# Booking SyncE's DMA issues at other lengths, and other distances for long transfers, in a kernel that plans its own order

## The chip, the cores and the metric

The kernel runs on one core of one Trainium2 chip. The metric is the device time in microseconds (us), and the median of several runs is given. One further execution is profiled; every duration of a single instruction comes from that one. The names of the engines are those of the profile: PE is the matmul engine (PEld its weight loads), DVE the vector engine, ACT the scalar engine, POOL the general-purpose engine, SP the engine that only issues DMA transfers. A "q" behind a name (SPq) means the engine's instruction queue.

## The reference

Two blocks follow one another: a delta-rule attention over 768 time steps for 4 batches x 8 heads of width 48, and a gated feed-forward network on its output.

```python
k_n = k / (np.linalg.norm(k, axis=-1, keepdims=True) + 1e-06)
state = np.zeros((B, H, D, D), dtype=np.float32)
for t in range(S):
    kt, vt, bt = (k_n[:, :, t], v[:, :, t], beta[:, :, t, None])
    y[:, :, t] = np.einsum('bhd,bhde->bhe', q[:, :, t], state)
    v_old = np.einsum('bhde,bhd->bhe', state, kt)
    state = state + bt[:, :, :, None] * np.einsum('bhd,bhe->bhde', kt, vt - v_old)
...
x = attn_out.transpose(0, 2, 1, 3).reshape(B * S, H * D)      # 3072 x 384
rms = np.sqrt(np.mean(x * x, axis=-1, keepdims=True) + 1e-06)
xn = x / rms * rms_g
g = xn @ w_gate                                               # 384 x 1536
silu = g * (1.0 / (1.0 + np.exp(-g)))
val = xn @ w_val
return (silu * val @ w_out).astype(np.float32)                # 1536 x 384
```

## The kernel before, in words

The sequence is cut into 12 chunks of 64 steps. For each chunk there are four kinds of work.

- `load` brings in `k`, `q` and `v` of the chunk. `weights` brings in the three weight matrices once, in 18 pieces of 768 KB, in the first quarter of the time; the core holds them as float32 after a conversion on ACT and DVE.
- `prep` makes the chunk's triangular inverse. The products of keys (L555, L662) go out to device memory as `dkk` and come back in another layout as `at`; `at` is scaled (L682) and combined (L709 to L719); a chain of 15 pairs of DVE instructions (L731, L737) inverts it; the result `acc` goes out as `dx` and `dxt` and comes back as `mt`, `x2bd` and `m1bd`; two merges on PE (L813, L837) finish it. For chunks 0 to 3 the scaling is done on DVE, after that on POOL.
- `recur` takes the state forward one chunk and makes the chunk's output `yn`: products with the state (L878), with the inverse (L924), with the masked scores (L938), the new state (L975), then the root mean square (squares L1012 on ACT, the power on POOL at L1024 and L1025, the scaling on ACT at L1040) and a transposition (L1046).
- `ffn` is the feed-forward network of the chunk: for chunks 0 and 1 in plain form (up L1118, down L1100), for the ten others in a form with fewer products (up L1211, with DVE L1221 and ACT L1223 and L1227 behind it; down L1268, with DVE L1260 and L1277), and at the end the stores of 96 KB from `tmp` to the output.

All of it, over all chunks, is put into one list of operations (class `Op`) before a single instruction is emitted. Each has an engine, a duration that the author booked, what it reads and writes, and a priority. The class `Plan` then looks for an order: `forward` plays the list through with these durations, engine by engine, always taking the operation that can start first; `backward` goes from the end to the start and sets new priorities from how late each operation may be; random shakes are added. This is done 110 times (`ROUNDS`), the order with the earliest planned end is kept, and the instructions are emitted in it. Each engine executes its instructions strictly in that order; across engines only data dependences hold one up. So a booked duration never takes time itself: it only decides in which place of its engine's queue an instruction stands.

A DMA transfer is an operation of SP (in the startup some are ACT's): `dur` is the time that the issue is booked for on SP, `work` the time that the transfer is booked for on the DMA engines, which `forward` treats as one server. A transfer is either short, that is, part of a chain that other work waits for (`dkk`, `at`, `dx`, `mt` and the like), or `bulk` (loads of inputs and weights). From the second round on, the planner knows when the short ones were issued in the round before (`op.past`), and holds a bulk transfer back if it would come too close ahead of one:

```python
if op.bulk:
    for t, _ in soon:
        if t >= max(server, s + FIRST) + clear * op.work:
            break
        if t > s:
            s = t + 0.01
```

`clear` is the factor from `CLEAR`; the rounds take its three values in turn (`CLEAR[k % len(CLEAR)]`). On PE, the first 62 us are filled up with matmuls of no use (L1368) between the real ones.

Of the kernel before, what the change touches and what calls it, by code (L numbers as in the profile page):

```python
# [28 lines left out]
SHAKE = 0.06  # L29
RING, LANES, FIRST, LAND = 2330, 8, 1.08, 0.9  # L30
WARM = 62.0
CLEAR = (1.0, 0.6, 1.4)


class Op:
# [249 lines left out]
def kernel(  # L285
# [57 lines left out]
    NK, NKQ = 3, 2  # L343
    k2 = sbt("k2", [128, 16, DP], NK)
    q2 = sbt("q2", [128, 16, DP])
    q2t = q2.rearrange("p x e -> p (x e)").rearrange("p (u g th e) -> p u g th e", u=8, g=2, th=2)
    q2k = [("q2", i) for i in range(16)]
    vt = sbt("vt", [128, 16, D])
# [38 lines left out]
    raw = [more[:, 1536 * i : 1536 * i + 1536].bitcast(I64) for i in range(NRAW)]  # L387
# [7 lines left out]
    dkk = [dram.tile([2, 2, 16, W, W], FP32, name=f"dkk{i}") for i in range(2)]  # L395
    dx = [dram.tile([2, 2, 16, W, W], FP32, name=f"dx{i}") for i in range(2)]
# [5 lines left out]
    A = lambda n: 0.2 + 0.0008 * n  # L402
    G = lambda n: 0.15 + 0.0022 * n

    def dma(dst, src, prio, r=(), w=(), work=0.2, dur=0.45, eng="SP", after=0.0, desc=256, bulk=False):
        queue = nc.scalar if eng == "ACT" else nc.sync
        op = P.add(eng, dur, lambda: queue.dma_start(out=dst, in_=src), prio, r, w, lat=0.1)  # L407
        op.dma, op.work, op.ready, op.desc, op.bulk = True, work, after, desc, bulk
        op.port = False
# [55 lines left out]
    def weights():  # L465
        todo = []
        for half_ in range(2):
            c0 = half_ * WCOL

            for i_ in range(3):  # L470
                for side, (key, w) in enumerate((("wg", moe_w_gate), ("wv", moe_w_val))):
                    c1 = c0 + 256 * i_
                    src = w.rearrange("(t p) c -> p t c", p=128)[:, :, c1 : c1 + 256]
                    todo.append((w_in[:, side, half_, i_:9:3], src, [(key, half_, i_)]))
                if i_:
                    for f in ((6 * half_,) if i_ == 1 else (6 * half_ + 2, 6 * half_ + 4)):
                        src = moe_w_out[f * 128 : f * 128 + 256, :].rearrange("(a p) c -> p a c", a=2)
                        z = spot(f)
                        todo.append((wo_sb[:, z : z + 2], src, [("wo", f), ("wo", f + 1)]))
        for n, (dst, src, keys) in enumerate(todo):  # L480
            pr = (30 if n < 9 else CV2) + 0.2 * n
            i, a = n % NRAW, n % NCV
            parts = dst.shape[1]
            rdst = raw[i].rearrange("p (a c) -> p a c", a=parts)
            dma(rdst, src, (0.1 if n == 0 else 3 + 2 * n), w=[("raw", i)], dur=0.45, work=3.06, desc=384 if parts == 3 else 256, bulk=True)

            low, high = (raw[i].bitcast(U32)[:, w_ : w_ + 2 * WCOL - 1 : 2] for w_ in range(2))
            top, cc = cva[a], cvb[a]
            cak, cvk = [("cva", a)], [("o", 1)] if a else [("tmp", 1), ("tmp", 2)]
            u, r = top.bitcast(U32), cc.bitcast(U32)  # L490
            tiled = lambda t: t.rearrange("p (a n) -> p a n", a=parts)

            P.add("ACT", 0.84, lambda high=high, top=top: nc.scalar.activation(out=top, in_=high.bitcast(FP32), func=ACTF.Prelu, scale=2.0**-112, alpha=2.0**32), pr, r=[("raw", i)], w=cak)
            P.add("ACT", 0.84, lambda low=low, r=r: nc.scalar.mul(r, low, 2.0**-29), pr, r=[("raw", i)], w=cvk)
            P.add("DVE", 0.57, lambda u=u: nc.vector.tensor_scalar(out=u, in0=u, scalar1=3, scalar2=None, op0=ALU.logical_shift_left), pr, w=cak)
            P.add("DVE", 0.93, lambda dst=dst, u=tiled(u), r=tiled(r): nc.vector.tensor_tensor(out=dst.bitcast(U32), in0=u, in1=r, op=ALU.add), pr, r=cvk + cak, w=[("cv", n)])
            done = [("cv", n)]
            for key in keys:
                ready.setdefault(key, []).extend(done)
# [4 lines left out]
    def load(c, what):  # L504
        t0 = c * C
        pk, pq, pv = ((-5, 1, 12), (5, 29, 36))[c] if c < 2 else (due(c, 150), due(c, 99), due(c, 70))
        if "q" in what and c > 1:
            for d, eh, g, th in itertools.product(range(2), repeat=4):
                e0, e1 = 32 * eh, min(D, 32 * eh + 32)
                src = q.rearrange("b (yh a) t e -> a t (b yh) e", a=4)[2 * d + g, t0 + 32 * th : t0 + 32 * th + 32, :, e0:e1]  # L510
                r0 = 64 * d + 32 * eh
                dma(q2t[r0 : r0 + 32, :, g, th, 0 : e1 - e0], src, pq, w=[q2k[8 * d + 4 * eh + 2 * g + th]], work=0.21, bulk=True)
        for key, t, src, pr in (("k2", k2[c % NK], k, pk), ("q2", q2, q, pq)):
            for g in range(2):
                if key[0] not in what or key == "q2" and c > 1:
                    continue
                dst = t[64 * g : 64 * g + 64, :, 0:D]
                s = src.rearrange("b (y g) t e -> g t (b y) e", g=2)[g, t0 : t0 + C]
                dma(dst, s, pr, w=[(key, c % NK, g)] if key == "k2" else q2k[8 * g : 8 * g + 8], dur=0.65, work=1.15, desc=1024, eng="ACT" if c == 0 and g and key == "k2" else "SP", bulk=c > 0 or key == "q2")
        if "v" in what:  # L520
            for bb in range(2):
                s = v[2 * bb : 2 * bb + 2, :, t0 : t0 + C, :].rearrange("p h t e -> t (p h) e")
                dma(vt[64 * bb : 64 * bb + 64], s, pv, w=[("v", bb)], dur=0.65, work=1.15, desc=1024, bulk=True)

    def turn(src, dst, keys, r, pr, split):

# [76 lines left out]
    def prep(c):  # L603
        early = c < 2
        pr = 8.0 if c == 1 else due(c, 110)
        if c == 0:
            pr = 0.0
        pn = pr if early else due(c, 125)
        pd = pr + (1 if c else 0)
        pi = (1.0, 45.0)[c] if c < 2 else due(c, 80)  # L610
        i2, ikq, ikk, imt = c % 2, c % NKQ, 2 if c == 1 else c % 2, int(c == 1)
# [6 lines left out]
        eng, e_ = (nc.vector, "DVE") if fast else (nc.gpsimd, "POOL")  # L618
# [3 lines left out]
        if c == 0:  # L622
# [3 lines left out]
            for d in range(2):  # L626
                dst = kraw[:, d:16:2]
# [24 lines left out]
            pr = 6.0  # L652
# [6 lines left out]
        for d in range(2):  # L659
            dst = kk[ikk][:, :, d:16:2]  # L660
            src = lambda d=d, ps=ps: ps[d].t.rearrange("p (u i t) -> p i u t", u=8, i=2)
            P.add("ACT", A(512), lambda dst=dst, f=src: nc.scalar.mul(dst, f(), -1.0), pr, r=[ps[d]], w=kkd(d), last=ps[d])  # L662

        dk = dkk[c % 2]
        for g in range(2):
            for i in range(2):
                r0 = 64 * g + W * i
                src = kk[ikk][r0 : r0 + W, i] if c else kraw[r0 : r0 + W, :, W * i : W * i + W]
                kbkeys = [(("kka", ikk // 2, d), ("kkb", ikk, d))[i] if c else ("kr", d) for d in range(2)]
                dma(dk[i, g].rearrange("x j t -> j x t"), src, pd, r=kbkeys, w=[("dkk", c % 2, g, i)], work=0.43, dur=0.4, desc=512, eng="ACT" if c == 0 and g else "SP")  # L670
        dkeys = [("dkk", c % 2, g, i) for g in range(2) for i in range(2)]
        at_, an = (at2, "at2") if c == 1 else (at1, "at")
        atk = [(an, 0), (an, 1)]
        for par in range(2):
            dma(at_[64 * par : 64 * par + 64].rearrange("p j t -> p (j t)"),
                dk.rearrange("i g x j t -> (i g x) (j t)"), pd, r=dkeys, w=[(an, par)], dur=0.5, work=1.42, desc=64, eng="SP" if par or c else "ACT")
        bt = beta_b[:, c]
        bkeys = [("beta", i) for i in range(8)]

# [24 lines left out]
        x, xkeys = (xs_[c + 1], [("xs", c)]) if early else (xs_[0], ["acc"])  # L704
# [21 lines left out]
        for j in range(0, W - 2, 2):  # L726
            n, m = j // 2 + 1, W - 2 - j
# [32 lines left out]
        turns = itertools.cycle(("SP",) if c else ("ACT", "SP"))  # L760
        for par in range(2):
            dst = dx[i2].rearrange("i g x (s two) t -> two (i g x) s t", two=2)[par]
            dma(dst, x[64 * par : 64 * par + 64], pi, r=xkeys, w=[("dx", i2, par)], dur=0.6, work=0.9, desc=1024, eng=next(turns))
            if early:
                continue
            dst = dxt[i2].rearrange("t g x s -> (g x) t s")[:, :, 16 * par : 16 * par + 16]
            dma(dst, xt_[64 * par : 64 * par + 32], pi, r=["acc"], w=[("dxt", i2, par)], dur=0.65, work=0.67, desc=1024)
        xk = [("dx", i2, 0), ("dx", i2, 1)]
        xtk = [("dxt", i2, 0), ("dxt", i2, 1)]
        for i in range(2):  # L770
            for bb in range(2):
                r0 = 64 * bb + W * i
                for g in range(2):
                    src = dx[i2][i, g, 8 * bb : 8 * bb + 8].rearrange("x s t -> s x t")
                    dma(mt[imt][r0 : r0 + W, 8 * g : 8 * g + 8, W * i : W * i + W], src, pi, r=xk, w=[("mt", imt, i, bb, g)], eng=next(turns))
        for y_ in range(4):
            src = dx[i2][1].rearrange("g (b y) s t -> y s (g b) t", y=4)[y_]
            dst = x2bd[W * y_ : W * y_ + W, :, y_]
            dma(dst, src, pi, r=xk, w=[("x2bd", y_)], eng=next(turns))
        if early:  # L780
# [13 lines left out]
            for g in range(2):  # L794
                s = slice(64 * g, 64 * g + W)
                for bb in range(2):
                    src = lambda s=s, bb=bb: psm[bb].t[s, 0:256].rearrange("p (x s) -> p x s", s=W)
                    dst = m1bd[s, 8 * bb : 8 * bb + 8, g]
# [4 lines left out]
        else:  # L803
            for g in range(2):
                src = dxt[i2][:, g]
# [598 lines left out]
```

## Time and profile before

| | |
|---|---|
| median of 3 runs | 707.42 us (703.76 to 709.53) |
| the profiled execution | 708.47 us |
| its span, first to last instruction | 706.7 us |
| instructions | 23129 |
| PE busy | 688.2 us, 97% of the span |
| DVE busy | 538.7 us, 76% |
| ACT busy | 314.9 us, 45% |
| POOL busy | 138.2 us, 20% |
| mean granted clock of PE | 0.99 |
| DMA | 54.66 MB, mean 77 GB/s; 0.79 of the engines' time before 64 us, 0.62 from 64 to 190 us, 0.19 after 560 us |
| DMA issues on SP | 556 |

The span is the profiled execution without the 1.8 us that lie around it. Busy time is not added up over engines, since they work side by side. Engine SP has no busy time in the table: its issues are seen in the timeline and among the instructions of line L407, where every transfer is made. A wait is written as "who waited <- who ended the wait: total us, times, longest us". In the timeline a row has the start, the length, the engine, the line, what was written from what, and in brackets the idle time before it with what ended it.

### The profile page before, as it was taken

The page shows a single profiled execution, that of the slowest core. Times are in us where ns is not written, and L with a number is a line of the kernel's source. Part 1 is how long each engine was busy: PE and PEld are TensorE (multiplying, and loading weights), DVE is VectorE, ACT ScalarE, POOL GpSimd, SP SyncE. Part 2 cuts the span into 40 slices and gives each one's busy share as a digit, 9 for nine tenths or more (in the row PEclk, how much of TensorE's full clock was granted, in tenths as well). Part 3 has the DMA queues.
Part 4 walks back from the last instruction along what each step waited for, and adds up shares of the span by engine and source line. Part 5 has one row for each costly group of instructions (what it writes and reads, how often), then busy time and mean ns, then how long its engine had stood idle before and what let it go on. Part 6 is the DMA issues. An engine that isn't in the chain of part 4 may idle for free.

```text
span 706.7 us, 23129 instructions
## 1 busy us (share of the span) xinstructions
PE 688.2 (97%) x9924; PEld 628.1 (89%) x9924; DVE 538.7 (76%) x1121; ACT 314.9 (45%) x720; POOL 138.2 (20%) x140
## 2 busy tenths in 40 slices
PE   8998999999999989999999999999998999999997
PEld 6567768787789989999999999999998999999997
DVE  4896993599999739959957966979955988957373
ACT  5247573562235345345355254355354255345241
POOL 6020040030503005032106005042104131100000
PEclk9999999999999999999999999999999999999999
DMA  7975978821541361164352264253153061040101
GB/s 116 186 176 112 225 178 194 210 49 17 95 79 25 62 99 31 28 104 69 60 94 28 38 95 86 39 103 51 34 79 57 2 114 29 18 62 2 23 1 23
DMA packets 232790, 54.66 MB, mean 77 GB/s; under 512 B 221936, under 2 KB 225008, under 8 KB 232688
## 3 DMA queue, kind: packets, MB, share of 16 engines
q1 hardware_dynamic: 227840, 52.27, 39.5%
q8 instruction: 78, 1.28, 0.8%
q10 hardware_dynamic: 4848, 0.92, 0.7%
q14 instruction: 24, 0.20, 0.1%
HBM read 40.83 MB, written 12.32 MB: 75 GB/s over the span
## 4 chain that ended last, share of the span: by engine, by line
PE 75%; DVE 11%; SPq 6%; DMA 3%; issue 2%; POOL 1%; ACT 1%; DVEq 0%; ACTq 0%; POOLq 0%
PE bank L1211 31%; PE bank L1268 16%; PE bank L1118 9%; SPq L407 6%; PE bank L1100 3%; PE bank L878 3%; DVE acc L737 3%; PE bank L555 2%; DVE acc L731 2%; PE bank L924 2%; PE bank L938 2%; PE bank L837 1%; PE bank L532 1%; PE bank L975 1%; PE bank L1368 1%
## 5 line engine op out<-in xcount | busy, mean ns | idle before, releaser
L1211 PE MATMUL bank<-xf,w_in 128*128 128x128 f32 x1440 | 180.3, 277 | 2.4 <-ACT tmp L1223 2.2
L1221 DVE TENSOR_TENSOR tmp<-tmp,bank 128x512 f32<-128x512 f32 x180 | 122.2, 684 | 78.2 <-PE bank L1211 58.7
L1211 PEld LDWEIGHTS bank<-xf,w_in 128*128 128x128 f32 x1440 | 169.6, 192 | 5.2 <-ACT tmp L1223 2.4
L1211 PE MATMUL bank<-xf,more 128*128 128x128 f32 x960 | 125.2, 278 | 1.2 <-DVE tmp L1221 1.2
L1211 PEld LDWEIGHTS bank<-xf,more 128*128 128x128 f32 x960 | 116.1, 193 | 3.4 <-DVE tmp L1221 1.9
L1223 ACT COPY tmp<-bank 128x512 f32<-128x512 f32 x120 | 69.4, 585 | 69.0 <-PE bank L1211 39.9
L1227 ACT ACTIVATE tmp<-tmp 128x256 f32<-128x256 f32 x120 | 49.7, 417 | 105.2 <-DVE tmp L1221 104.7
L737 DVE TENSOR_REDUCE acc<-acc 128x30 f32<-128x90 f32 (+4 forms) x180 | 85.1, 473 | 6.2
L577 POOL TENSOR_TENSOR knrm<-ksum,half 128x16 f32<-128x16 f32 x12 | 36.1, 3009 | 157.1 <-DVE ksum L576 157.1
L1268 PE MATMUL bank<-wo_sb,hf 128*128 128x192 f32 x360 | 63.9, 327 | 0.2 <-ACT kt L544 0.2
L1228 DVE TENSOR_TENSOR hf<-tmp 128x256 f32<-128x256 f32 x120 | 51.4, 443 | 14.1 <-ACT tmp L1227 13.6
L731 DVE TENSOR_TENSOR acc<-acc,at 128x60 f32<-128x60 f32 (+4 forms) x165 | 58.2, 353 | 4.2 <-POOL at L714 1.7
L1268 PEld LDWEIGHTS bank<-wo_sb,hf 128*128 128x128 f32 x360 | 58.2, 190 | 0.7 <-ACT kt L544 0.5
L758 POOL COPY acc<-acc 128x128 f32<-128x128 f32 x40 | 18.2, 486 | 140.3 <-DVE acc L737 139.4
L1368 PE MATMUL bank<-ident 128*128 128x128 f32 (+2 forms) x148 | 43.5, 439 | 1.4 <-POOL ident masks.py:199 1.4
L1368 PEld LDWEIGHTS bank<-ident 128*128 128x128 f32 x148 | 25.0, 198 | 17.9 <-issue 15.4
L682 POOL TENSOR_TENSOR at<-at,beta_b 128x1024 f32<-128x1024 f32 x8 | 18.9, 2360 | 104.4 <-DMA q<-in_q_dram 49.5
L1100 PE MATMUL bank<-wo_sb,hf 128*128 128x384 f32 x96 | 34.0, 490 | 0.0
L1118 PE MATMUL bank<-xf,w_in 128*128 128x256 f32 x144 | 33.9, 385 | 0.0
L1118 PE MATMUL bank<-xp,w_in 128*128 128x256 f32 x144 | 33.6, 389 | 0.0
L1118 PEld LDWEIGHTS bank<-xp,w_in 128*128 128x128 f32 x144 | 28.1, 197 | 5.0
L1118 PEld LDWEIGHTS bank<-xf,w_in 128*128 128x128 f32 x144 | 26.7, 190 | 4.7 <-issue 0.2
(166 smaller groups left out, 997.3 us busy)
## 6 DMA issues: line engine op xcount, KB each, us to landing
at<-dkk SPq DMA_DIRECT2D x21, 256.0 KB, 4.0
vt<-in_v_dram SPq DMA_DIRECT2D x24, 192.0 KB, 4.1
more<-in_moe_w_val_dram SPq DMA_DIRECT2D x6, 768.0 KB, 8.2
more<-in_moe_w_gate_dram SPq DMA_DIRECT2D x6, 768.0 KB, 5.7
more<-in_moe_w_out_dram SPq DMA_DIRECT2D x6, 768.0 KB, 6.9
out_dram<-tmp SPq DMA_DIRECT2D x48, 96.0 KB, 2.2
k<-in_k_dram SPq DMA_DIRECT2D x23, 192.0 KB, 4.3
mt<-dx SPq DMA_DIRECT2D x84, 32.0 KB, 2.1
```

The costliest lines, as they stand in the source:

```text
L407: op = P.add(eng, dur, lambda: queue.dma_start(out=dst, in_=src), prio, r, w, lat=0.1)
L731: nc.vector.tensor_tensor(out=acc[:, 1:3, 0:n, j + 2 : W].rearrange("p a i t -> p i a t"), in0=acc[:, old, 0:n, j : j + 2, None].to_broadc ...
L737: nc.vector.tensor_reduce(out=acc[:, new, 0:n, j + 2 : W], in_=acc[:, lo : lo + 3, 0:n, j + 2 : W].rearrange("p a i t -> p i t a"), axis=A ...
L1100: nc.tensor.matmul(po[p].t[:, 0:DM], hf[:, spot(f), 128 * p : 128 * p + 128], wo_sb[:, spot(f)], start=(f == f0), stop=(f == f1 - 1), skip ...
L1118: nc.tensor.matmul(ps.t[:, TOK * side : TOK * side + TOK], w_in[:, side, h_, 3 * t + i_, n : n + 128], x_[:, 2 * t : 2 * t + 2].rearrange( ...
L1211: nc.tensor.matmul(g.t[:, 128 * z : 128 * z + 128], fac[:, side, 128 * f : 128 * f + 128], xf[:, xs], start=(begin and z == 0), stop=False ...
L1221: P.add("DVE", V(512), lambda t=t, g=g: nc.vector.tensor_tensor(out=t, in0=t, in1=g.t, op=ALU.add), -1, r=[g], w=[tk], last=g)
L1223: P.add("ACT", A(512), lambda t=t, g=g: nc.scalar.copy(t, g.t), -1, r=[g], w=[tk], last=g)
L1227: P.add("ACT", A(256), lambda t=t: nc.scalar.activation(out=t[:, 0:256], in_=t[:, 0:256], func=ACTF.Silu), -1, w=[tk])
L1228: P.add("DVE", V(256), lambda t=t, f0=f0, p=p: nc.vector.tensor_tensor(out=hf[:, spot(f0) : spot(f0) + 2, 128 * p : 128 * p + 128], in0=t[ ...
L1268: nc.tensor.matmul(g.t[:, 0:192], a_[:, f], b_[:, f], start=(begin and f == 0), stop=(f == 5), skip_group_check=True)
L1368: nc.tensor.matmul(warm[:, 0 : 128 * w_].rearrange("p (w n) -> p w n", n=128), ident, ident[:, None, :].to_broadcast([128, w_, 128]))
```

## The change

The booked issue times on SP go up, each kind of transfer to a figure of its own, and the three distances become smaller. No operation is added, removed or given other data. The order is planned anew with the new figures, so that any instruction on any engine can change its place.

```diff
-CLEAR = (1.0, 0.6, 1.4)
+CLEAR = (0.5, 0.8, 1.1)
...
-    def dma(dst, src, prio, r=(), w=(), work=0.2, dur=0.45, eng="SP", after=0.0, desc=256, bulk=False):
+    def dma(dst, src, prio, r=(), w=(), work=0.2, dur=0.53, eng="SP", after=0.0, desc=256, bulk=False):
...
-            dma(rdst, src, (0.1 if n == 0 else 3 + 2 * n), w=[("raw", i)], dur=0.45, work=3.06, ...)      # weights
+            dma(rdst, src, (0.1 if n == 0 else 3 + 2 * n), w=[("raw", i)], dur=0.55, work=3.06, ...)
...
-                dma(dst, s, pr, w=..., dur=0.65, work=1.15, desc=1024, ...)                                  # k, early q
+                dma(dst, s, pr, w=..., dur=0.7, work=1.15, desc=1024, ...)
...
-                dma(vt[64 * bb : 64 * bb + 64], s, pv, w=[("v", bb)], dur=0.65, work=1.15, ...)
+                dma(vt[64 * bb : 64 * bb + 64], s, pv, w=[("v", bb)], dur=0.7, work=1.15, ...)
...
-                dma(dk[i, g]..., src, pd, r=kbkeys, w=[("dkk", c % 2, g, i)], work=0.43, dur=0.4, ...)
+                dma(dk[i, g]..., src, pd, r=kbkeys, w=[("dkk", c % 2, g, i)], work=0.43, dur=0.5, ...)
...
-                dk.rearrange(...), pd, r=dkeys, w=[(an, par)], dur=0.5, work=1.42, desc=64, ...)             # at
+                dk.rearrange(...), pd, r=dkeys, w=[(an, par)], dur=0.56, work=1.42, desc=64, ...)
...
-            dma(dst, x[64 * par : 64 * par + 64], pi, r=xkeys, w=[("dx", i2, par)], dur=0.6, work=0.9, ...)
+            dma(dst, x[64 * par : 64 * par + 64], pi, r=xkeys, w=[("dx", i2, par)], dur=0.65, work=0.9, ...)
```

The default of `dma` holds for `mt`, `x2bd`, `m1bd`, the pieces of `q` from chunk 2 on, `beta` and the output stores. `dxt` stays at 0.65.

## The prediction, made before the change was run

> **What bounds the kernel now.** I read the busy table first, then the table of stages, then the waits of PE.
>
> ```profile
> PE 688.2 (97%) x9924; PEld 628.1 (89%) x9924; DVE 538.7 (76%) x1121; ACT 314.9 (45%) x720; POOL 138.2 (20%) x140
> ```
> ```profile
> 236.00:262.00 26.00, 23.78 (x316) 22.92 (x314) 12.02 (x24) 9.58 (x22) 1.53 (x4) 0.93 0.53 88
> 262.00:530.00 268.00, 266.80 (x4285) 258.76 (x4283) 213.64 (x459) 124.44 (x296) 64.86 (x65) 1.00 0.38 62
> 530.00:560.00 30.00, 27.53 (x483) 26.27 (x482) 21.71 (x42) 12.47 (x32) 11.16 (x9) 0.94 0.19 35
> ```
> The columns are stretch, length, busy PE, PEld, DVE, ACT, POOL, granted clock, DMA share, GB/s. From 262 to 530 us PE is busy 266.8 of 268 us, and no order of the same matmuls makes that shorter. What an order can give back sits in short places such as the other two rows, where PE pauses and the clock is below 1.00. The waits of PE name them:
>
> ```profile
> PE bank L1046 <- ACT yn L1040: 2.5, 1, 2.5
> PE bank L1211 <- ACT tmp L1223: 2.2, 1, 2.2
> PE bank L924 <- issue: 2.1, 1, 2.1
> PE bank L878 <- issue: 1.6, 1, 1.6
> ...
> PE bank L924 <- DMA mt<-dx: 0.6, 1, 0.6
> ```
> A pause costs more than itself. Stretches of 2 us behind the two longest pauses (length, busy PE, clock):
>
> ```profile
> 258.00:260.00 2.00, 2.00 (x38) 0.50 0.58 88
> ...
> 548.00:550.00 2.00, 2.00 (x56) 0.50 0.00 0
> ```
> Together with the partial rows around them (0.72 and 0.93; 0.75 and 0.89) each dip loses 2 x (0.28 + 0.50 + 0.07) = 1.7 us, the second 2 x (0.25 + 0.50 + 0.11) = 1.7 us, of full clock. So these two pauses cost 2.2 + 1.7 = 3.9 us and 2.5 + 1.7 = 4.2 us. The Trainium skill, "TensorE: Matmul & The Clock Gate", Part 1, says the array falls to half clock after at least one idle window of some 3.4 us. Pauses of 2.2 and 2.5 us did it here, so the trace decides; by the page's figure each pause would cost itself alone, and the gain below would be some 3.0 us smaller.
>
> **Why PE paused.** The timeline around the first one, SyncE's issues and what waited:
>
> ```profile
> 244.53 1.27 SPq L407 DMA_DIRECT2D dx<-acc  x2
> 245.84 0.79 SPq L407 DMA_DIRECT2D q<-in_q_dram  x1
> 246.73 2.30 SPq L407 DMA_DIRECT2D dkk<-kk  x4
> 249.07 1.06 SPq L407 DMA_DIRECT2D m1bd<-dxt  x2
> 250.18 1.82 SPq L407 DMA_DIRECT2D x2bd<-dx  x1
> 252.10 1.14 SPq L407 DMA_DIRECT2D out_dram<-tmp  x2
> ...
> 254.98 1.07 ACT L1223 COPY tmp<-bank 128x512 f32<-128x512 f32 x2 [4.11 <-DMA out_dram<-tmp]
> ...
> 256.11 0.38 PE L1211 MATMUL bank<-xf,w_in 128*128 128x128 f32 x1 [2.22 <-ACT tmp L1223]
> ```
> SP issues without a break, and the store of a finished output tile is the eleventh in line. The `tmp` buffer that it reads is wanted by ACT's next copy; the store lands at 254.9, ACT has idled 4.1 us, the banks that it should have emptied are not free, PE stops. The other pause has the same root: SP issues from 510.0 to 536.9, its `at` loads come near the end, POOL starts on `at` (L682) at 539.26, and behind that work, on the same POOL queue, stands the power of L1025, which ACT (L1040) and then PE (L1046) need. In both, SP is late.
>
> **The change, part by part.** (1) It alters nothing that runs: the same 556 issues on SP, the same matmuls, the same tiles. Instructions added: none, so direct cost 0. (2) It raises what the planner books per issue: 0.45 to 0.53 for `mt`, `x2bd`, `m1bd`, `out` and late `q`; 0.45 to 0.55 for weights; 0.40 to 0.50 for `dkk`; 0.50 to 0.56 for `at`; 0.60 to 0.65 for `dx`; 0.65 to 0.70 for `k` and `v`. The trace has (minimum/median/maximum, ns):
>
> ```profile
> L407 SPq DMA_DIRECT2D q<-in_q_dram x164: 311/449/5347, 14.7 to 536.5; - x164
> L407 SPq DMA_DIRECT2D mt<-dx x84: 303/449/2093, 41.1 to 630.3; - x84
> L407 SPq DMA_DIRECT2D out_dram<-tmp x48: 466/592/636, 176.2 to 703.6; - x48
> L407 SPq DMA_DIRECT2D dkk<-kk x40: 302/499/1232, 53.4 to 568.5; - x40
> ```
> The medians plus some 0.05 us between two issues are the new figures or a little less; single issues of 1.2 to 5.3 us stay unbooked. Now the two bursts. From 244.53 to 252.10, ten issues took 7.57 us. Booked before: 2 x 0.60 + 0.45 + 4 x 0.40 + 2 x 0.45 + 0.45 = 4.60. Booked after: 1.30 + 0.53 + 2.00 + 1.06 + 0.53 = 5.42. The planner's error falls from 2.97 to 2.15 us. From 510.0 to 535.2, 41 issues took 25.2 us; booked before 4 x 0.45 (out) + 14 x 0.45 (q) + 2 x 0.65 + 2 x 0.60 + 14 x 0.45 (m1bd, x2bd, mt) + 4 x 0.40 + 0.50 = 19.0, after 22.1. The error falls from 6.2 to 3.1 us.
>
> What that is worth at the places themselves, if the planner fills the corrected time as tightly as before: the first pause shrinks by 0.8 us to 1.4 us. No clock dip follows the shortest pauses in the list (0.6), one follows 1.6; at 1.4 it may go either way, so the saving is 0.8 at the low end and the whole 3.9 at the high end (the stores simply go first). I take 3.2, nearer the high end, because ten transfers with later users stand ahead of one whose user is already late. The second: the error shrinks by 3.1 us, more than the 2.5 us pause, so all 4.2. The wait on `mt` at 481 (0.6) goes likewise. Sum 8.0 us, ends 5.6 and 8.7.
>
> (3) The distances. CLEAR multiplies a long transfer's time; before a short transfer that the last round planned, a bulk one starts only if that much time is left, and otherwise waits until behind it. The rounds take three values in turn: they change from 1.0, 0.6, 1.4 to 0.5, 0.8, 1.1, on average 1.0 to 0.8, so loads may sit closer to the chain's transfers. The trace shows no run with other distances. From below: a gain of up to the other pauses, 1.6 + 1.7 at 104 us, where PE stands within one group of matmuls with no releaser shown and the DMA engines full. From above, the nearest row of a load in bad company (single issues at 72 us, then the page's row for all):
>
> ```profile
> k<-in_k_dram SPq DMA_DIRECT2D x2, 192.0 KB, 10.5
> ```
> ```profile
> k<-in_k_dram SPq DMA_DIRECT2D x23, 192.0 KB, 4.3
> ```
> Issued right behind three weight loads, `k` lands after 10.5 instead of 4.3 us, 6.2 us late. That one was hidden: its first user starts at 90.9. For a chain transfer it would not be. The planner's forward pass also charges a bulk transfer's time to the ones behind it, so I take neither end but one new pause of 1.4 us without a dip, the size that a burst's remaining error leaves.
>
> Sum: the profiled execution took 708.47 us (span 706.7 and 1.8 around it). 708.47 - 8.0 + 1.4 = 701.9. It lies 1.05 above the median of the runs, 707.42, so the forecast is 700.8, rounded **701 us**. Its own range is 697 to 705.
>
> **Rivals.** *No net change, 707 us.* For it: the long single issues (1.82 us at 250.18) are still not booked, so pauses of the same size turn up elsewhere: 3.9 + 4.2 back. Against it: the bursts' error does halve. The Trainium skill, "DMA: Bandwidth & Descriptors", section "Issuing engines are not separate DMA queues", speaks for it too: it calls the time to start a transfer usually small relative to the transfer. Here one `mt` issue takes 0.45 us and lands in 2.1, but eight in a row take 3.9 to 4.0 us, so in bursts the trace contradicts it.
>
> *A larger gain, 695 us.* Both queue pauses go whole (3.9 + 4.2 + 0.6) and so does the one at 104 us (1.6 + 1.7): 12.0 below 707.4. For it: better figures help at every chunk, and with PE as full as from 262 to 530 everywhere nothing else is needed. Against it: that third pause is not SP's.
>
> *Slower, 715 us.* The smaller distances put a bulk load ahead of a chain transfer in the startup. There the chain of waits alternates between DVE steps and single transfers (`at` lands 4.8 us after issue at 13.8), and PE runs fillers until its first product, L1118, at 68 us; from there it is full, so each us by which L1118 starts later counts whole. Priced by the `k` row: 6.2 late and one dip of 1.7, and in this case nothing won later: 715.3. It decides from 6.6 us on, an L1118 that starts after 74.7 us, for that eats the gain above. For it: 0.8 of the DMA engines' time is taken before 64 us, and the smallest distance falls from 0.6 to 0.5. Against it: 0.8 and 1.1 are tried too, and the order with the earliest planned end is kept.
>
> **How the numbers follow.** Forecast 0.40, half of it below 700.3 (1% under the median; 1% is about what a measurement of this kernel can tell from no change). Larger gain 0.18, no net change 0.14, slower 0.28. Faster by over 1%: 0.20 + 0.18 = 0.38; within 1%: 0.20 + 0.14 = 0.34; slower: 0.28. The range goes to 693 (the larger gain and the 2.1 us pause at 53 us as well) and to 719 (the slower case with one pause of 3.9 added).
>
> **What would show it.** Right: PE's waits on `tmp` L1223 and `yn` L1040 under 1 us each, two fewer stretches at clock 0.50 after 200 us, `out` stores ahead of `m1bd` and `x2bd` in SP's bursts, matmul counts per line unchanged, the first L1118 at 66 to 70 us. Wrong in the distances: a DMA named as what ended a PE or DVE wait before 75 us, or chain transfers that land over 6 us after issue. Wrong in the bursts: the same count of dips with other names. The prediction fails as a whole if the end is set by a chain that holds no SP issue, or if the startup moves by more than 5 us either way.

## The result, and the profile after

In a series of 20 runs of each kernel in turn the changed kernel takes 702.2 us (median), the one before 705.88. The ratio is 0.9951, with a 95% interval of 0.9932 to 0.9969: 3.5 us, or half a per cent, faster. The profiled execution has a span of 700.9 us instead of 706.7.

The busy table, from the page of the changed kernel:

```profile
PE 685.0 (98%) x9930; PEld 624.4 (89%) x9930; DVE 529.2 (76%) x1121; ACT 311.6 (44%) x720; POOL 135.4 (19%) x140
```
The six more matmuls of PE are fillers of the first 62 us (L1368 has 154 instead of 148). The work is the same; it lies closer together. The waits of PE:

```profile
PE bank L1118 <- DVE w_in L496: 3.7, 2, 2.5
PE bank L1211 <- DVE tmp L1221: 2.1, 3, 1.2
...
PE bank L532 <- DMA q<-in_q_dram: 1.3, 1, 1.3
```
Both pauses of the prediction are gone, and so is the wait of 0.6 us on `mt` (L924) near 481 us. The table of stages at the old places of the two pauses (length, then PE, PEld, DVE, ACT, POOL, granted clock, DMA share, GB/s) shows PE full and the clock whole:

```profile
236.00:262.00 26.00, 26.00 (x292) 25.61 (x292) 17.20 (x38) 10.19 (x25) 8.00 (x9) 1.00 0.51 90
...
530.00:560.00 30.00, 30.00 (x612) 28.80 (x612) 26.73 (x61) 11.66 (x31) 11.13 (x9) 1.00 0.14 24
```
The timeline of SyncE's issues (SP in the rows) gives the reason for the first:

```profile
241.71 0.65 SPq L407 DMA_DIRECT2D dxt<-acc  x1
242.40 1.36 SPq L407 DMA_DIRECT2D out_dram<-tmp  x2
244.15 0.83 SPq L407 DMA_DIRECT2D x2bd<-dx  x2
245.09 0.93 SPq L407 DMA_DIRECT2D m1bd<-dxt  x2
```
The stores now stand ahead of `x2bd` and `m1bd`. For the second, SP issues `at` at 527.6 us, where it did so at 533.9 before; the timeline of SP, of POOL and of PE:

```profile
527.64 1.91 SPq L407 DMA_DIRECT2D at<-dkk  x2
...
532.70 2.36 POOL L682 TENSOR_TENSOR at<-at,beta_b 128x1024 f32<-128x1024 f32 x1 [24.06 <-DMA at<-dkk]
...
539.09 0.71 POOL L1025 TENSOR_TENSOR rs<-ms,mhalf 128x2 f32<-128x2 f32 x1
...
543.82 0.82 PE L1046 MATMUL bank<-ident,yn 128*128 128x128 f32 x6
```
POOL begins on `at` at 532.7 instead of 539.3, the power L1025 runs at 539.1 instead of 545.7, and PE reaches L1046 without a wait.

What is new is a wait in the startup: a weight load, issued at 71.7, lands after 8.0 us, and the chain of conversions behind it holds up the first products.

```profile
79.83 0.90 ACT L493 ACTIVATE more<-more 128x768 f32<-128x768 f32 x1 [5.88 <-DMA more<-in_moe_w_gate_dram]
...
84.23 1.13 PE L1118 MATMUL bank<-xf,w_in 128*128 128x256 f32 x4 [2.49 <-DVE w_in L496]
```

**Where the time came from.** Two orders are hard to compare by the clock, since the same matmuls stand in other places. So I counted work: each matmul that is no filler weighs the median distance between two starts of its form in the profile of before (0.112 us for L1211, 0.163 for L1268, and so on; 605 us in all), and for each kernel the table says how much later (+) or earlier (-) than before it has done the same amount, in its profiled execution. Other fair weights for the small matmuls would move most entries by 0.5 us or less.

| work done, us | before is at | after | e1 | e2 | e3 | e4 | e9 |
|---|---|---|---|---|---|---|---|
| 90 | 151.1 | +0.8 | +7.0 | -4.6 | +0.1 | -2.6 | -2.3 |
| 180 | 246.1 | +0.5 | +5.7 | -4.0 | -0.1 | -2.9 | -2.1 |
| 195 | 266.7 | -4.5 | +3.8 | -9.0 | -3.4 | -5.2 | -5.6 |
| 300 | 377.0 | +0.6 | +4.7 | 0.0 | +0.9 | -3.5 | -4.8 |
| 450 | 537.7 | -1.7 | +3.5 | +7.5 | -0.1 | -4.6 | -6.9 |
| 465 | 557.2 | -5.5 | -0.6 | +3.4 | +3.6 | -8.8 | -11.0 |
| 600 | 697.2 | -5.8 | -0.7 | +4.9 | +3.5 | -6.6 | -10.9 |

The changed kernel gains 5.0 us at the first pause (180 to 195), gives all of it back by 300, and gains 2.3 us from 300 to 450 and 3.8 at the second pause (450 to 465), which it keeps. The columns e1 to e9 are the experiments.

A column also holds what differs between two executions of the same order. e4, described below, issues on every engine exactly what the kernel before issues up to 539 us, and yet its profiled execution is 4.6 us ahead at 450: its pauses near 55, 105 and 254 us last 1.0, 1.2 and 1.4 us instead of 2.1, 1.6 and 2.2, and none of them brings half clock. So a step at one place can be read, but a total of a column is good to some us only.

### The profile page after: what moved, and what is told of

It is laid out like the page before. It is cut to its first block, busy times and chain, and to the rows that moved or that the text cites. A ratio compares the mean times of both kernels' runs of the same rounds, so it can differ in the third digit from the quotient of the medians.

```text
span 700.9 us, 23147 instructions
## 1 busy us (share of the span) xinstructions
PE 685.0 (98%) x9930; PEld 624.4 (89%) x9930; DVE 529.2 (76%) x1121; ACT 311.6 (44%) x720; POOL 135.4 (19%) x140
## 4 chain that ended last, share of the span: by engine, by line
PE 73%; DVE 14%; DMA 5%; SPq 3%; POOL 2%; issue 2%; ACT 2%; DVEq 0%; POOLq 0%; ACTq 0%
PE bank L1211 32%; PE bank L1268 18%; PE bank L1118 5%; PE bank L1100 3%; PE bank L555 3%; SPq L407 3%; PE bank L878 2%; PE bank L1368 2%; DMA more<-in_moe_w_gate_dram 2%; DVE tmp L1221 2%; DVE acc L737 2%; DVE acc L731 2%; PE bank L532 2%; PE bank L924 1%; PE bank L837 1%
## 5 line engine op out<-in xcount | busy, mean ns | idle before, releaser
L1211 PE MATMUL bank<-xf,w_in 128*128 128x128 f32 x1440 | 181.0, 277 | 0.0
L1221 DVE TENSOR_TENSOR tmp<-tmp,bank 128x512 f32<-128x512 f32 x180 | 120.9, 683 | 74.6 <-PE bank L1211 57.1
L1211 PEld LDWEIGHTS bank<-xf,w_in 128*128 128x128 f32 x1440 | 170.5, 192 | 3.0 <-issue 1.2
L1211 PE MATMUL bank<-xf,more 128*128 128x128 f32 x960 | 124.6, 277 | 2.1 <-DVE tmp L1221 2.1
L1211 PEld LDWEIGHTS bank<-xf,more 128*128 128x128 f32 x960 | 115.3, 192 | 4.2 <-DVE tmp L1221 3.2
L1268 PE MATMUL bank<-wo_sb,hf 128*128 128x192 f32 x360 | 64.3, 328 | 0.0
L731 DVE TENSOR_TENSOR acc<-acc,at 128x60 f32<-128x60 f32 (+4 forms) x165 | 59.1, 358 | 6.6 <-POOL at L714 4.4
L1268 PEld LDWEIGHTS bank<-wo_sb,hf 128*128 128x128 f32 x360 | 58.1, 190 | 0.5
L1228 DVE TENSOR_TENSOR hf<-tmp 128x256 f32<-128x256 f32 x120 | 49.8, 431 | 11.0 <-ACT tmp L1227 10.4
L1368 PE MATMUL bank<-ident 128*128 128x128 f32 (+2 forms) x154 | 45.3, 440 | 1.4 <-POOL ident masks.py:199 1.4
L1368 PEld LDWEIGHTS bank<-ident 128*128 128x128 f32 x154 | 26.2, 197 | 18.4 <-issue 15.7
L1118 PE MATMUL bank<-xf,w_in 128*128 128x256 f32 x144 | 34.9, 386 | 4.1 <-DVE w_in L496 3.7
L1118 PEld LDWEIGHTS bank<-xf,w_in 128*128 128x128 f32 x144 | 26.4, 190 | 10.4 <-DVE w_in L496 4.5
L1118 PE MATMUL bank<-xp,w_in 128*128 128x256 f32 x144 | 33.1, 382 | 0.4 <-DVE hf L1126 0.4
L1118 PEld LDWEIGHTS bank<-xp,w_in 128*128 128x128 f32 x144 | 27.0, 190 | 5.4 <-DVE hf L1126 0.5
```

Source lines behind the costliest of these rows:

```text
L731: nc.vector.tensor_tensor(out=acc[:, 1:3, 0:n, j + 2 : W].rearrange("p a i t -> p i a t"), in0=acc[:, old, 0:n, j : j + 2, None].to_broadc ...
L1118: nc.tensor.matmul(ps.t[:, TOK * side : TOK * side + TOK], w_in[:, side, h_, 3 * t + i_, n : n + 128], x_[:, 2 * t : 2 * t + 2].rearrange( ...
L1211: nc.tensor.matmul(g.t[:, 128 * z : 128 * z + 128], fac[:, side, 128 * f : 128 * f + 128], xf[:, xs], start=(begin and z == 0), stop=False ...
L1221: P.add("DVE", V(512), lambda t=t, g=g: nc.vector.tensor_tensor(out=t, in0=t, in1=g.t, op=ALU.add), -1, r=[g], w=[tk], last=g)
L1228: P.add("DVE", V(256), lambda t=t, f0=f0, p=p: nc.vector.tensor_tensor(out=hf[:, spot(f0) : spot(f0) + 2, 128 * p : 128 * p + 128], in0=t[ ...
L1268: nc.tensor.matmul(g.t[:, 0:192], a_[:, f], b_[:, f], start=(begin and f == 0), stop=(f == 5), skip_group_check=True)
```

## The experiments

**The two pauses by themselves.** e3 and e4 keep the order of before and move one thing by hand after the planning. (The edit adds six lines, so line numbers above 270 are six higher.)

```diff
+MOVED = (("SP", (211, 212, 213), 215),)            # e3: two m1bd and one x2bd go behind two output stores
+MOVED = (("POOL", (69, 70, 71, 72), 73),)          # e4: four steps on at go behind the power of the root
...
-        for op, s in best[1]:
+        rows = best[1]
+        for eng, moved, last in MOVED:
+            mine = [x for x in rows if x[0].eng == eng]
+            late, at = [mine[k] for k in moved], rows.index(mine[last])
+            rows = [x for x in rows[: at + 1] if x not in late] + late + rows[at + 1 :]
+        for op, s in rows:
```

> The order of before with one thing moved: in SP's burst at 244 to 256 us the two output stores go ahead of two m1bd and one x2bd transfers. If the pause at 254 us is SP's lateness and PE is the bound behind it, the pause and its half-clock stretch go: 2.2 + 1.7 = 3.9 us less, 0.9945. If the time won there is given back later, as the lead of the changed kernel over before is between 262 and 377 us, 1 us less or nothing: 0.999 to 1.000.

Measured: 706.63 us against 706.84, ratio 1.0004 (0.9976 to 1.0033). No gain. The store does go first and the pause does go: in the table, e3 leads by 3.4 us at 195. But by 300 it is 0.9 behind. The timeline of e3:

```profile
263.65 2.36 POOL L688 TENSOR_TENSOR at<-at,beta_b 128x1024 f32<-128x1024 f32 x1 [23.04 <-DMA q<-in_q_dram]
...
264.33 3.89 DVE L1234 TENSOR_TENSOR hf<-tmp 128x256 f32<-128x256 f32 x2
...
272.32 0.38 PE L1217 MATMUL bank<-xf,more 128*128 128x128 f32 x1 [2.39 <-DVE tmp L1227]
```
Two DVE multiplications take 3.89 us. In the timeline of before the same two (L1228) take:

```profile
267.73 0.79 DVE L1228 TENSOR_TENSOR hf<-tmp 128x256 f32<-128x256 f32 x2
```
POOL's work on `at` starts when `at` has landed, which SP decides: at 263.4 in before, at 263.7 in e3, whether PE has paused or not. Without the pause, DVE comes to these multiplications 3.4 us sooner, and so while POOL is still in its first two long steps. Each then takes 2.0 instead of 0.4 us: they end at 266.3 and 268.2, just behind POOL's two steps, which end at 266.0 and 267.9. PE runs dry for 2.4 us, and the half clock follows. In this execution the pause had been hiding a collision, and one that is no data dependence: two engines also hold each other up without one. (The profiled execution, 711.99 us, is the longest of e3's twelve; the median too says no gain, but how much of that each run pays in this way is not shown.) The Trainium skill, "SBUF — State Buffer", section "Who interferes with whom", says that a DVE instruction with two inputs in SBUF, the memory on the chip where the tiles lie, contends with a POOL instruction that reads SBUF, for ports that one of the two locks. The 2.0 us beside POOL and the 0.4 us without it agree with that. In the changed kernel POOL does these four steps from 242.3 to 248.3 us, out of the way.

> The order of before with one thing moved: on POOL at 539 us the power of the root mean square (L1024, L1025) goes ahead of the four scaling and combining steps on at (L682 to L714). If POOL's queue behind the late at is what stops PE at 544.6 us, the pause and its half-clock stretch go: 2.5 + 1.7 = 4.2 us less, 0.994. If the end is set by the chain through at itself (L682, then the DVE steps), which starts 1.4 us later here, no gain, 1.000.

Measured: 703.17 us, ratio 0.9950 (0.9924 to 0.9976), 3.5 us less (1.7 to 5.4): the first theory, within its interval. One exchange on POOL's queue is worth as much as the whole change. The timeline and the stage of e4:

```profile
535.43 0.71 POOL L1031 TENSOR_TENSOR rs<-ms,mhalf 128x2 f32<-128x2 f32 x1
536.12 2.61 POOL L688 TENSOR_TENSOR at<-at,beta_b 128x1024 f32<-128x1024 f32 x1
...
539.87 0.82 PE L1052 MATMUL bank<-ident,yn 128*128 128x128 f32 x6
```
```profile
530.00:560.00 30.00, 28.08 (x543) 26.90 (x542) 26.43 (x54) 10.56 (x28) 12.23 (x9) 1.00 0.12 24
```
The clock stays whole. PE still loses 1.9 us here, 1.7 of it in a wait on DVE (`xp` L1266); the table has 4.2 won and 2.2 given back right behind it. The 2.0 that are left in this one execution are fewer than the 3.5 of the medians, but within their interval.

**The two halves of the change.** e1 has the new issue times with the old distances, e2 the old issue times with the new distances.

```diff
-CLEAR = (0.5, 0.8, 1.1)      # e1, from the changed kernel
+CLEAR = (1.0, 0.6, 1.4)
...
-CLEAR = (1.0, 0.6, 1.4)      # e2, from the kernel before
+CLEAR = (0.5, 0.8, 1.1)
```

> The new issue times with the old distances (1.0, 0.6, 1.4). If the booked issue times carry the gain, 0.995 of before (some 3.5 us less), and no stretch at half clock behind a queue pause after 200 us. If the distances carry it, 1.000 and queue pauses of 2 us and more remain. If any new order is just another draw, anything from 0.99 to 1.01 with pauses at other places.

Measured: 707.43 us, ratio 1.0006 (0.9980 to 1.0033). After 190 us PE has no wait but 1.9 us on DVE, and no half clock until the end, as the first theory wants; yet the time is that of before. The loss is in the startup, in this stage:

```profile
64.00:100.00 36.00, 32.42 (x527) 25.08 (x520) 31.99 (x66) 18.81 (x38) 5.96 (x7) 0.91 0.71 162
```
Before, PE was busy all 36 us there at clock 1.00. By work, e1 is 7.0 us late at 90 and wins that back later, 4.1 of it at the second pause.

> The old issue times with the new distances (0.5, 0.8, 1.1). If the booked issue times carry the gain, no faster than before (1.000 or more), with SP bursts booked 3 to 6 us short and at least one PE pause of over 1.5 us and its half-clock stretch after 200 us. If the distances carry it, 0.995.

Measured: 714.84 us, ratio 1.0117 (1.0074 to 1.0160): slower by 8.0 us. The startup is quick here (4 us ahead at 180), and the first pause is gone, but the second has come back elsewhere, larger, in the same form: POOL's power behind POOL's work on `at`.

```profile
PE bank L1046 <- ACT yn L1040: 3.7, 1, 3.7
```
```profile
496.88 0.71 POOL L1025 TENSOR_TENSOR rs<-ms,mhalf 128x2 f32<-128x2 f32 x1
497.63 1.12 ACT L1040 ACTIVATE yn<-yn,rs 128x384 f32<-128x384 f32 x2 [4.49 <-POOL rs L1025]
```
POOL's last step on `at` (L714) runs from 495.15 to 496.49, right ahead of the power. So the parts, +0.1 and +1.2%, do not add up to the whole, -0.5%. Either is an order of its own with its own pauses.

**How much is the draw?** The planner shakes its priorities at random. Another number in `random.Random(47)` gives another order from the same figures.

```diff
-        rng = random.Random(47)
+        rng = random.Random(48)      # and 49
```

> The kernel before with other random shakes of the priorities (random.Random(48) for 47): same bookings, same distances, another order. If the bookings and distances decide the time, 0.998 to 1.002 of before. If each order is a draw, anything from 0.99 to 1.012, with its pauses at other places than 254 and 545 us.

> As e5 with random.Random(49): 0.998 to 1.002 of before if bookings and distances decide; 0.99 to 1.012 if each order is a draw.

> The changed kernel with other random shakes (48 for 47). If the new bookings and distances together carry the gain, 0.993 to 0.997 of before again and PE pauses behind an SP burst under 1.5 us. If the changed kernel's order was a good draw, 0.998 to 1.012.

> As e7 with random.Random(49): 0.993 to 0.997 of before if bookings and distances carry the gain; 0.998 to 1.012 if the order was a good draw.

Measured: e5 714.94 us, ratio 1.0090 (1.0062 to 1.0118); e6 708.92, 1.0012 (0.9991 to 1.0034); e7 707.44, 0.9987 (0.9956 to 1.0017); e8 716.35, 1.0104 (1.0070 to 1.0137). Bookings and distances alone do not fix the time: the changed figures give 0.9951, 0.9987 and 1.0104, the old ones 1, 1.0090 and 1.0012. An order is a draw with a spread of about one per cent, and the change moves the time by half of one.

**What the bookings do.** In every unbroken run of at least nine SP issues I took the length in the trace less the booked lengths, per issue. With the old times it is 0.173 us (before), 0.154 (e2), 0.177 (e5), 0.193 (e6); with the new ones 0.079 (after), 0.078 (e1), 0.118 (e7), 0.106 (e8). The planner sees SP more truly. What that could be worth is the choice among draws, and so the last four kernels leave the choice to the planner: of 40 further numbers, the two whose order it expects to end first, with the new figures (e9, e10) and with the old ones (e11, e12).

```diff
-        rng = random.Random(47)
+        rng = random.Random(62)      # e9, and 77 in e10, in the changed kernel; 83 in e11 and 73 in e12, in the one before
```

> The changed kernel with the shakes (62) whose order the planner itself found best of 40 other shakes. If truer bookings make the planner's choice worth more, 0.990 to 0.995 of before, at or below the changed kernel. If each order is a draw, 0.995 to 1.010 like the others.

> As e9 with the shakes second in the planner's own ranking (77): 0.990 to 0.995 if truer bookings make the choice worth more, 0.995 to 1.010 if each order is a draw.

> The kernel before, its old bookings and distances, with the shakes (83) that its planner ranks first of the same 40. If the old bookings make the choice worth less, 0.998 to 1.005; if bookings do not matter, the same 0.990 to 1.010 as e9 and e10, on either side of them. In SP's bursts the trace is longer than booked by 0.15 us and more per issue here, by 0.12 and less in e9 and e10.

> As e11 with the shakes second in the ranking (73): 0.998 to 1.005 if the old bookings make the choice worth less, 0.990 to 1.010 on either side of e9 and e10 if bookings do not matter.

Measured: e9 698.42 us, ratio 0.9891 (0.9866 to 0.9917); e10 700.50, 0.9921 (0.9896 to 0.9947); e11 705.01, 0.9972 (0.9946 to 0.9998); e12 712.74, 1.0083 (1.0052 to 1.0114). The bursts: 0.101 and 0.079 us per issue, against 0.150 and 0.184. The two that the planner chose with the new figures are faster than the three others with them (by chance alone that happens in one case of ten); the two chosen with the old figures (0.997, 1.008) are no better than the three others with those (1, 1.009, 1.001). e9 beats both kernels. Its stages:

```profile
350.00:530.00 180.00, 180.00 (x2906) 174.54 (x2905) 144.39 (x311) 85.09 (x202) 45.86 (x44) 1.00 0.38 63
530.00:680.00 150.00, 150.00 (x1926) 146.90 (x1925) 102.98 (x214) 60.37 (x147) 11.75 (x17) 1.00 0.17 30
```
From 350 to 680 us PE has no idle time at all. Over all kernels the five with the new times and distances (after, e7 to e10) average 0.997 and the five with the old ones (before, e5, e6, e11, e12) 1.003, with a spread of 0.8 and 0.5% within the two groups; that difference alone is not beyond chance (some 0.4% standard error). The ranking within the groups is the stronger sign, and two chosen orders a side are few. The new times and the new distances go together in it; e9 and e10 do not separate them.

The planned ends themselves say more (`self.end` of `Plan`, which the code of each kernel computes before an instruction is emitted). With the new figures they are 684.4, 685.0, 686.6, 688.5 and 691.0 us for e9, e10, after, e7 and e8, and the measured times have the same order. With the old ones they are 684.2, 684.2, 685.3, 685.6 and 690.4 us for e11, e12, before, e6 and e5, and the measured times have the same order but for e12. So an early planned end is a good sign with either set of figures. That it is a better one with the new set rests on few orders and is not shown.

## Why the prediction was right, and where it was not

The forecast was 701 us with a range of 697 to 705 of its own, and the median is 702.2. Against the kernel before, it named 6.4 us, and 3.5 came. That the time lies so near is in part luck: the kernel before measured 1.5 us less in this series than in the one forecast from, and the same new figures with two other random numbers take 0.9987 and 1.0104 of before (e7, e8). By its steps:

- **PE is full, and pauses are all that an order can give back.** Right in the main: e9, the fastest, has no idle time of PE from 350 to 680 us, and most of the changed kernel's gain that lasts lies at one pause.
- **The second pause, 4.2 us, and the wait on `mt`, 0.6.** Right: 3.8 us at the place of the pause by work, and e4, which removes it alone, measures 3.5 (1.7 to 5.4). The wait on `mt` is gone as well; no run prices it alone.
- **The first pause, 3.2 us.** The term that was mis-sized: the pause goes, as forecast, because the stores go first, but e3 measures nothing won (1.0004; by its interval 1.7 us at most). In part its size hung on one execution: of the 3.9 us that the prediction read at this pause, 1.7 were a stretch of half clock that e4's execution, with the same order there, does not have. The step behind it was that PE is the bound wherever it is not paused, so that a pause removed is time kept. What stood next was DVE behind POOL's work on `at`, whose start SP sets. The changed kernel, too, has given those 5.0 us back by 300 us of work. Two waits of PE on DVE are 2.0 of them: 1.2 at 310.6 us (L1221), and 0.8 at 342.7, where a DVE step (L731) took 1.70 us instead of 0.42 beside POOL's L654. Where the rest went is not shown.
- **SP's bursts, an error cut by half or a quarter.** Right for the whole kernel: 0.173 to 0.079 us per issue.
- **The distances, one new pause of 1.4 us.** The form of the step was wrong. Distances alone cost 8.0 us (e2), the issue times alone nothing (e1), both together gain 3.5. A part of such a change has no price that could be put into a sum, since every part gives a whole new order. The prediction priced repairs of the old order and took the rest as unchanged; the spread of one per cent between draws (e5 to e8) belonged in it as a term, and it would have been as large as the sum.
- **The slower case.** The startup did get worse where it said, at loads that land late, but at a weight load: L1118 began at 68.4 us, within the 66 to 70 given, and lost 3.7 us soon after. By 90 us of work all but 0.8 was made good, so not every us that is lost there counts whole. The two signs that were named for wrong distances do not tell the kernels apart: PE waits on a transfer before 75 us in both (1.3 on `q` and 0.7 on `wsum` in the changed kernel, 0.6 on `q` and 0.3 on `mt` in the one before), and the slowest transfer to or from `dx` lands after 6.5 and 8.0 us.
- **No net change.** Its argument, pauses of the same kind at other places, is what e1 and e2 show. The changed kernel escaped it; that its bookings are the reason is made likely by e9 to e12 and not shown for this one order.

## What to carry to other kernels

Before a gain is booked for a removed pause, look at what the next engine does in the time behind it: a transfer's landing that does not move with PE can put another engine's work just where the time was won. Where a planner makes a whole new order, run it with a few other random numbers first; only what is larger than their spread says anything about the figures. Choosing the earliest planned end among many orders gave the fastest kernel here (e9, 0.989; but also e12, 1.008, with the old figures), and it costs no change of the kernel; that truer figures make this choice better is likely, not shown.

## What the runs showed of the hardware

The half clock of PE does not follow a pause by a fixed rule of length. In the changed kernel a pause of 2.5 us costs no clock (stretches of 2 us: length, busy PE, clock, DMA share, GB/s):

```profile
82.00:84.00 2.00, 0.00 (x0) 1.00 1.05 320
84.00:86.00 2.00, 1.77 (x52) 1.00 0.66 104
```
In before one of 1.6 us, at 106 us, is followed by 3.41 us of half clock. In e3 one of 3.4 us, which ends at 548.1, goes with half clock for 10.24 us from 546.8 on, of which these rows show the last part:

```profile
552.00:554.00 2.00, 2.00 (x51) 0.50 0.04 8
554.00:556.00 2.00, 2.00 (x8) 0.50 0.00 0
556.00:558.00 2.00, 2.00 (x11) 0.73 0.00 0
```
The granted clock's records have stretches of 3.41 us (four in before, behind pauses of 1.6 to 2.5 us), 6.83 (e5, e8) and 10.24 (e3), one, two and three times the same unit, and none in the changed kernel until the last matmuls. The 6.83 us at 103.8 us in e8 come with no single pause over 0.8 us near them. The starts of the stretches, too, lie whole units apart, while the pauses do not: in before they begin 51.2, 150.2 and 290.1 us after one another, 15, 44 and 85 times 3.413. The Trainium skill, "TensorE: Matmul & The Clock Gate", Part 1, says that the window by which the clock is set is 3413 ns long and runs freely, without a new start when a kernel begins. The units and the starts agree with it. So part of what a single profile shows for a pause, 1.7 us in before and about 4.5 in e3, depends on where it falls. e4, with the order of before, has no half clock at 105 and 254 us, though its pauses there are shorter too (1.2 and 1.4 us). The sum of the prediction had counted the second pause's 1.7 us as certain, and most of the first's.
